# A recurrent attention and an MLP on one core: preparation once a chunk on dense tiles, moved within SBUF

## The chip, the cores and the metric

One core of a Trainium2 chip runs the kernel. Its engines work in parallel, each in the order of its own instructions, and wait for each other by semaphores: TensorE (PE; its weight loads are listed as PEld), VectorE (DVE), ScalarE (ACT), GpSimd (POOL) and SyncE (SP). SP does no arithmetic here: it issues DMAs, in order, and a DMA whose buffer is not yet free holds up all that stand behind it. GpSimd issues DMAs too. The metric is the device time in microseconds (us), lower is better.

## The reference, cut to what matters

A state of 40 x 40 for each of 4 batches and 8 heads is carried over 768 time steps; the outputs of all heads go through an MLP with Mish.

```python
# r, k, v, w, a, b: (4, 8, 768, 40)
for t in range(768):
    y[:, :, t] = einsum('bhd,bhde->bhe', rt, state)
    Sa = einsum('bhde,bhe->bhd', state, at)
    state = state * wt[:, :, None, :] - einsum('bhd,bhe->bhde', Sa, bt) \
            + einsum('bhd,bhe->bhde', vt, kt)
x = y.transpose(0, 2, 1, 3).reshape(3072, 320)
h = x @ w_in                                   # 320 -> 2048
g = h * tanh(softplus(h))                      # Mish
out = g @ w_out                                # 2048 -> 320
```

## The kernel before, in words

The 768 steps are cut into 12 chunks of 64 steps (C = 64, `nch` = 12). Within a chunk the recurrence is written with products: `P`, the running product of w, scales a; `E`, the products from the other end, scale b and k; and a 32 x 32 triangular inverse for each of 32 systems gives the effect of the Sa term. A chunk has 32 (batch, head) pairs. They are treated as two halves (`be` = 0, 1) of 16 pairs; in a half, `al` = 0, 1 stands on partitions 0 to 39 and 64 to 103, eight pairs s beside each other. So 80 of 128 partitions carry data.

The stages, by function:

- `pre_a(c, be)` prepares a half chunk. SP loads w and a (`wa`) and b and k (`bk`), VectorE forms the product of the first half of w (L145), the scan P (L147), a times P (L152), the scan E (L157) and b, k times E (L170). ScalarE copies a into a block-diagonal tile `ad` (L155). TensorE multiplies `ad` with `bk` (L186) and transposes `bk` (L202); ScalarE and VectorE bring the results into `GP` and `HA` (L188 to L193, the masks are VectorE's). Once a chunk TensorE moves the two ends of P to both halves (L166, with parts of the identity) into `RW`. GpSimd stores P to DRAM (`pD`, L172), since the MLP's input is y times P.
- `pre_inv(n)` inverts for two chunks at once: VectorE alone, from a transpose into `XL` (L209) over thirty pairs of product and sum (L214, L216) to a transpose into `TT` (L218) and one into GP (L220). `post_inv(n)` goes on with it on TensorE (L232, L241, L258).
- `step(c)` runs the recurrence of a chunk: products L284, L293, L304, L314, L334, L339, with VectorE at L316, L342, L346. GpSimd loads v and r for it.
- The MLP takes 256 rows for each chunk: products with w_in (L585), Mish, products with w_out (L605 to L607). Its weights arrive as pairs of 32-bit words, and are converted in parts: a DMA (`cv_d`, SP), ScalarE (L459), VectorE (L461 to L463), ScalarE (L494) and VectorE (L495). w_in takes twelve such parts of 512 columns. With `NQ0 = 1` three of them are converted at the program's start (`early`), into tiles of their own, the other nine when preparation's buffers are free (`first`), with one buffer (`CVA = 1`); w_out follows (`second`, `third`).

`ORDER` and `LA` set that preparation runs two pairs of chunks ahead of the steps. The order of the instructions on each engine is then set by a scheduler with its own estimate of durations; `OFF` shifts the priority of each part. `QS` names the engines that issue the DMAs of loads, step loads, outputs and P.

Of the kernel before, what the change touches and what calls it, by code (L numbers as in the profile page):

```python
# [7 lines left out]
F32 = mybir.dt.float32  # L8
# [10 lines left out]
NWA = 2  # L19
# [8 lines left out]
QS = "SGGG"  # L28
# [9 lines left out]
OFF = {'I': 80, 'T1': 80, 'P00': -40, 'P10': 80, 'P11': 40, 'b0': 15, 'c0': 600, 'u0': -15, 'u1': 250, 'd0': 250,  # L38
# [9 lines left out]
def layouts(inp, S=768):  # L48
# [7 lines left out]
    wt = w.transpose(4, 2, 1, 6, 3, 0, 5).reshape(nch, 2, 2, 40, 8, C)  # L56
    wa = np.zeros(wt.shape[:4] + (1040,), np.float32)
    wa[..., :520].reshape(wt.shape[:4] + (8, 65))[..., 1:] = wt
    wa[..., 528:] = a.transpose(4, 2, 1, 6, 3, 0, 5).reshape(nch, 2, 2, 40, 512)
    o['wa'] = wa  # L60
    bt, kt = (x.transpose(4, 2, 1, 6, 3, 0, 5).reshape(nch, 2, 2, 40, 8, 1, C) for x in (b, k))
    bk = np.concatenate([bt, kt], -2)
    bk[:, 1] = np.concatenate([kt, bt], -2)[:, 1]
    o['bk'] = bk.reshape(nch, 2, 2, 40, 8, 128)
# [4 lines left out]
    cst = np.zeros((128, 328), np.float32)  # L69
# [4 lines left out]
    cst[:, 296:328] = np.arange(32) < p[:, None] % 32  # L74
    o['cst'] = cst
# [3 lines left out]
def attention(ctx, tc, I, yD, pD, nch, M):  # L79
# [16 lines left out]
    cst = cs.tile([128, 328], F32, name="cst")  # L96
# [4 lines left out]
    wab = [cp.tile([128, 1040], F32, name=f"wa{i}") for i in range(NWA)]  # L101
    bkb = [cp.tile([128, 8, 168], F32, name=f"bk{i}") for i in range(NWA)]
    adb = [cp.tile([128, 8, 2, 2, 32], F32, name=f"ad{i}") for i in range(NAD)] * (2 // NAD)
    d1 = cp.tile([128, 584], F32, name="d1")
# [3 lines left out]
    for w, b in zip(wab, bkb):  # L108
        V.memset(w, 1.0)
        G.memset(b, 0.0)  # L110
    for t in [d1] + [x.rearrange("p s k a t -> p (s k a t)") for x in adb[:NAD]]:
        A.copy(t, z.broadcast_to(t.shape))
# [10 lines left out]
    RW, W2, HA, BKN, GP, KT = {}, {}, {}, {}, {}, {}  # L123
    LQ, SQ, OQ, PQ = (dict(S=SP, G=G, A=A)[x] for x in QS)

    def pre_a(c, be):
        n = 2 * c + be
        wa, bk, ad = wab[n % NWA], bkb[n % NWA], adb[n % 2]
        for al in range(2):
            q = slice(al * 64, al * 64 + 40)  # L130
            LQ.dma_start(out=wa[q], in_=I['wa'][c, be, al])
        for al in range(2):
            q = slice(al * 64, al * 64 + 40)
            LQ.dma_start(out=bk[q, :, 0:128], in_=I['bk'][c, be, al])
# [278 lines left out]

I32 = mybir.dt.int32
NH = 4
NQ0 = 1
NQ1 = 4
NO1 = 3
CVW = 512
# [240 lines left out]
```

## Time and profile before

| | us |
|---|---|
| median of 3 runs | 846.35 (843.54 to 848.62) |
| profiled execution | 842.54 |
| its span | 840.7 |
| TensorE busy, matmuls | 737.5 (88%) |
| VectorE busy | 463.3 (55%) |
| ScalarE busy | 427.9 (51%) |
| GpSimd busy | 103.3 (12%) |

In a line of the profile, L147 is a line of the kernel, `out<-in` are tiles without their buffer numbers, `x24` is the number of instructions, and behind the bar stand busy us, mean ns of one, and the idle time of the engine just before them with what ended it. Matmuls of 32-bit data are recorded twice, so eight products of a program show as x16. Granted clock 1.00 is TensorE's full speed; over the execution it was 0.947.

### The profile page before, as it was taken

Reading aid. Unit: us, or ns where it says so; the run is one execution under the profiler, and the core shown is the slowest. Engines: PE = TensorE matmul, PEld = TensorE weight load, DVE = VectorE, ACT = ScalarE, POOL = GpSimd, SP = SyncE. Lnnn points to the kernel's source line nnn. Section 1 sums busy time; section 2 is a strip of 40 time slices with the busy share of each in tenths; the row PEclk is TensorE's granted clock in tenths of the full one; section 3 lists DMA queues with packets and bytes.
Section 4 is the critical chain, followed back from the end, with each engine's and each line's share of the span. In section 5 each row is a group of like instructions: output and inputs, shape, how many; then the busy total and the mean of one; then the engine's idle time right before and its main releaser. Section 6 shows DMA issues by size and latency. Waiting matters only on the chain.

```text
span 840.7 us, 18817 instructions
## 1 busy us (share of the span) xinstructions
PE 737.5 (88%) x7816; PEld 688.5 (82%) x7816; DVE 463.3 (55%) x975; ACT 427.9 (51%) x937; POOL 103.3 (12%) x182
## 2 busy tenths in 40 slices
PE   2545898998989889888749999999999999999998
PEld 2444687887778778777648899999999999999998
DVE  6789889659879758947962649221222222122110
ACT  4533657774665766676457646333333333333331
POOL 8100021132123023211210200000000000000000
PEclk9755699899999999999978999999999999999999
DMA  6422232333333133313543744211120121100000
GB/s 173 139 72 64 82 78 67 96 75 94 89 96 88 57 86 98 96 26 98 139 123 82 186 132 127 54 39 32 38 54 29 26 54 36 35 20 16 16 1 32
DMA packets 58213, 61.92 MB, mean 74 GB/s; under 512 B 25536, under 2 KB 48704, under 8 KB 58128
## 3 DMA queue, kind: packets, MB, share of 16 engines
q1 hardware_dynamic: 49296, 40.94, 17.4%
q0 software_dynamic: 8832, 19.79, 9.4%
q8 instruction: 61, 1.00, 0.5%
q14 instruction: 24, 0.20, 0.1%
HBM read 48.79 MB, written 11.86 MB: 72 GB/s over the span
## 4 chain that ended last, share of the span: by engine, by line
PE 61%; ACT 15%; DVE 15%; DMA 5%; issue 4%; SPq 0%; POOL 0%; ACTq 0%; DVEq 0%
PE ph L585 20%; PE po L605 7%; PE po L606 7%; PE po L607 6%; PE pa L186 4%; PE pa L258 3%; PE pq L314 3%; PE pq L334 2%; DMA cv_d<-in_wi 2%; DVE XL L216 2%; DVE tmp L214 2%; ACT KT L260 2%; ACT bdT L250 1%; ACT bdT L249 1%; ACT ad L155 1%
## 5 line engine op out<-in xcount | busy, mean ns | idle before, releaser
L585 PE MATMUL ph<-xh,w_ih 128*128 128x256 f32 x576 | 148.9, 283 | 0.0
L587 ACT ACTIVATE g<-ph 128x512 f32<-128x512 f32 x96 | 57.3, 598 | 179.7 <-PE ph L585 179.7
L591 DVE TENSOR_TENSOR gl<-g,gh 128x1024 fp32r<-128x1024 f32 x48 | 58.6, 1224 | 160.3 <-ACT gh L590 160.0
L585 PE MATMUL ph<-xh,w_il 128*128 128x256 f32 x576 | 123.7, 283 | 0.0
L186 PE MATMUL pa<-bk,ad 128*128 128x168 f32 x384 | 85.5, 372 | 42.2 <-DVE bk L170 15.0
L606 PE MATMUL po<-w_ol,gh 128*128 128x320 f32 x384 | 118.6, 309 | 0.0
L607 PE MATMUL po<-w_oh,gl 128*128 128x320 f32 x384 | 118.3, 309 | 0.0
L605 PE MATMUL po<-w_oh,gh 128*128 128x320 f32 x384 | 117.8, 309 | 0.1
L585 PEld LDWEIGHTS ph<-xh,w_ih 128*128 128x128 f32 x576 | 109.5, 190 | 0.2 <-issue 0.2
L186 PEld LDWEIGHTS pa<-bk,ad 128*128 128x128 f32 x384 | 70.4, 232 | 47.6 <-issue 23.1
L585 PE MATMUL ph<-xl,w_ih 128*128 128x256 f32 x384 | 100.7, 284 | 0.0
L585 PEld LDWEIGHTS ph<-xh,w_il 128*128 128x128 f32 x576 | 96.2, 190 | 0.1
L585 PEld LDWEIGHTS ph<-xl,w_ih 128*128 128x128 f32 x384 | 73.1, 190 | 0.2 <-issue 0.2
L605 PEld LDWEIGHTS po<-w_oh,gh 128*128 128x128 f32 x384 | 71.8, 188 | 0.6 <-ACT w_oh L494 0.5
L606 PEld LDWEIGHTS po<-w_ol,gh 128*128 128x128 f32 x384 | 72.1, 188 | 0.2 <-DVE w_ol L495 0.2
L607 PEld LDWEIGHTS po<-w_oh,gl 128*128 128x128 f32 x384 | 72.1, 188 | 0.0
L216 DVE TENSOR_TENSOR XL<-XL,tmp 128x30 f32<-128x30 f32 (+9 forms) x180 | 58.8, 326 | 2.6
L214 DVE TENSOR_TENSOR tmp<-XL 128x30 f32<-128x30 f32 (+9 forms) x180 | 58.2, 323 | 2.6
L314 PE MATMUL pq<-bdr,UVT 128*128 128x128 f32 x384 | 55.2, 288 | 4.6 <-DVE UVQ L316 3.8
L258 PE MATMUL pa<-bdT,HA 128*104 128x128 f32 x384 | 52.7, 289 | 7.1 <-ACT bdT L251 4.8
L258 PEld LDWEIGHTS pa<-bdT,HA 128*104 128x104 f32 x384 | 47.2, 181 | 10.3 <-ACT bdT L251 5.9
L314 PEld LDWEIGHTS pq<-bdr,UVT 128*128 128x128 f32 x384 | 48.6, 197 | 7.0 <-DVE UVQ L316 4.9
(89 smaller groups left out, 1237.3 us busy)
## 6 DMA issues: line engine op xcount, KB each, us to landing
wa<-in_wa SPq DMA_DIRECT2D x48, 162.5 KB
bk<-in_bk SPq DMA_DIRECT2D x48, 160.0 KB
cv_d<-in_wi SPq DMA_DIRECT2D x12, 512.0 KB
cv_d<-in_wo SPq DMA_DIRECT2D x8, 640.0 KB
pD<-P POOLq DMA_DIRECT2D x48, 81.2 KB, 2.4
VS<-in_vN POOLq DMA_DIRECT2D x24, 160.0 KB, 3.3
UVT<-in_vD POOLq DMA_DIRECT2D x24, 160.0 KB, 4.0
bdr<-in_rD POOLq DMA_DIRECT2D x24, 160.0 KB, 4.5
```

The costliest lines, as they stand in the source:

```text
L186: PE.matmul(pt[:, j], ad[:, s0 + j].rearrange("p k a t -> p (k a t)"), bk[:, s0 + j], start=(j == 0), stop=True, skip_group_check=True)
L214: V.tensor_tensor(out=tv, in0=X[:, i + 1:32, i:i + 1].broadcast_to([128, 31 - i, i]), in1=X[:, i:i + 1, 0:i].broadcast_to([128, 31 - i, i] ...
L216: V.tensor_tensor(out=X[:, i + 1:32, 0:i], in0=X[:, i + 1:32, 0:i], in1=tv, op=ALU.add)
L258: PE.matmul(pk[:, j], ha[:, s0 + j], bd[:, s0 + j].rearrange("p a t -> p (a t)"), start=(j == 0), stop=True, skip_group_check=True)
L260: A.copy(kt[:, s0:s0 + 4], pk)
L314: PE.matmul(pq[:, s], UVT[:, g * 4 + s, be * 128:be * 128 + 128], br[:, be, g * 4 + s].rearrange("p a t -> p (a t)"), start=(s == 0), stop ...
L585: PE.matmul(o, w, x, start=(j == 0 and n == 0), stop=(n == 7), skip_group_check=True)
L587: A.activation(g[:, f0:f0 + 2], ph, AF.Mish)
L591: V.tensor_tensor(out=gl, in0=g, in1=gh.bitcast(F32), op=ALU.subtract)
L605: PE.matmul(po[k], gh[:, j, t], oh, start=(f == 0), stop=False, skip_group_check=True)
L606: PE.matmul(po[k], gh[:, j, t], ol, start=False, stop=False, skip_group_check=True)
L607: PE.matmul(po[k], gl[:, j, t], oh, start=False, stop=(f == 15), skip_group_check=True)
```

## The change

Preparation's work on VectorE is done once a chunk instead of once a half. `pre_d(c)` loads w, a, and b with k as dense tiles of 120 partitions and 11 blocks of 64 steps: three of the four groups of eight pairs (g = 2 be + al = 0, 1, 2) stand on partitions 0 to 39, 40 to 79 and 80 to 119, and the fourth group is spread over the three as blocks 8 to 10 (`wz`, `ax`, `bx`; two buffers each). The reduction, both scans and both products run on these. Then SP moves the results into the tiles that TensorE reads, by DMAs from SBUF to SBUF: six parts of a (into `a0`, `a1`, L178 of the new kernel) and six of b and k (into `bk0`, `bk1`, L184). P is stored by six DMAs a chunk instead of four (L193), and six selection products take the place of four (L189). The ScalarE copies, TensorE's products, the inverse and the steps stay as they were.

The MLP's weights are no longer converted early (`NQ0 = 0`): all twelve parts of w_in come in `first`, with two buffers (`CVA = 2`). `E` has a tile of its own, and the loads have a priority (`'L': 300`).

```diff
-NWA = 2
+NWZ = 2
+NAX = 2
+NBX = 2
+NE = 1
-QS = "SGGG"
+QS = "SGGGS"
...
-    def pre_a(c, be):
-        n = 2 * c + be
-        wa, bk, ad = wab[n % NWA], bkb[n % NWA], adb[n % 2]
-        for al in range(2):
-            q = slice(al * 64, al * 64 + 40)
-            LQ.dma_start(out=wa[q], in_=I['wa'][c, be, al])
-        for al in range(2):
-            q = slice(al * 64, al * 64 + 40)
-            LQ.dma_start(out=bk[q, :, 0:128], in_=I['bk'][c, be, al])
+    def parts():
+        for g in range(3):
+            yield g // 2, g % 2, slice(g * 40, g * 40 + 40), 0, 0, 8
+        for i in range(3):
+            yield 1, 1, slice(i * 40, i * 40 + 40), 8, 3 * i, min(3, 8 - 3 * i)
+
+    def pre_d(c):
+        wz = pw.tile([120, 716], F32, name="wz", bufs=NWZ)
+        a = pw.tile([120, 704], F32, name="ax", bufs=NAX)
+        bk = pw.tile([120, 11, 2, 64], F32, name="bx", bufs=NBX)
+        with at(tc, 'L'):
+            LQ.dma_start(out=wz, in_=I['wd'][c])
+            LQ.dma_start(out=a, in_=I['ad'][c])
+            LQ.dma_start(out=bk.rearrange("p s x t -> p (s x t)"), in_=I['bkd'][c])
...
+        V.tensor_reduce(out=w2[:, 0], in_=wz[:, 0:715].rearrange("p (s j) -> p s j", j=65)[:, :, 1:33], axis=AX.X, op=ALU.mult)
+        V.reciprocal(d1[:, 64:779:65], w2[:, 0])
+        V.tensor_tensor_scan(out=P, data0=wz[:, 0:715], data1=d1[:, 64:779], initial=0.0, op0=ALU.mult, op1=ALU.add)
...
         V.tensor_tensor(out=a3, in0=a3, in1=P3[:, :, 0:64], op=ALU.mult)
+        for be, al, q, h, s, m in parts():
+            DQ.dma_start(out=ab[be][al * 64:al * 64 + 40, s * 64:(s + m) * 64], in_=a[q, h * 64:(h + m) * 64])
+        V.reciprocal(d1[:, 64:779:65], w2[:, 1])
+        V.tensor_tensor_scan(out=E[:, 0:714][:, ::-1], data0=wz[:, 2:716][:, ::-1], data1=d1[:, 1:715][:, ::-1],
+                             initial=0.0, op0=ALU.mult, op1=ALU.add)
+        V.tensor_tensor(out=bk, in0=bk, in1=E3[:, :, 0:64].unsqueeze(2).broadcast_to([120, 11, 2, 64]), op=ALU.mult)
+        for be, al, q, h, s, m in parts():
+            DQ.dma_start(out=bkb[be][al * 64:al * 64 + 40, s:s + m, 0:128], in_=bk[q, h:h + m].rearrange("p s x t -> p s (x t)"))
+
+        RW[c] = wk.tile([128, 2, 16], F32, name="rw", bufs=4)
+        pt = ps_g.tile([128, 2, 2, 8], F32, name="pa")
+        for be, al, q, h, s, m in parts():
+            PE.matmul(pt[be * 64:be * 64 + 64, al, :, s:s + m], sel[:, q.start // 40], w2[:, :, h:h + m],
+                      start=(al == 0), stop=True, skip_group_check=True)
+        A.copy(RW[c], pt.rearrange("p a h s -> p a (h s)"))
+        for be, al, q, h, s, m in parts():
+            PQ.dma_start(out=pD[c, be, :, al, s * 65:(s + m) * 65], in_=P[q, h * 65:(h + m) * 65])
+
+    def pre_a(c, be):
+        if be == 0:
+            pre_d(c)
+        a, bk, ad = ab[be], bkb[be], adb[be]
...
-NQ0 = 1
+NQ0 = 0
...
-CVA = 1
+CVA = 2
```

The scheduler places the instructions anew. Line numbers of the new kernel from the inverse on are 29 higher than those of the old one (XL is L238, TT L247). On VectorE, ahead of the first inverse, there stood the last half of chunk 1 (`wa_97`, `bk_99`), a conversion (L461 to L495) and the masks (L191, L193); `w_689` belongs to chunk 2:

```order
L170 TENSOR_TENSOR bk_99<-bk_99,wa_97 128x8x128
L461 TENSOR_SCALAR cv_w<-cv_m 128x512
L462 SCALAR_TENSOR_TENSOR cv_w<-cv_m,cv_w 128x512
L463 SCALAR_TENSOR_TENSOR cv_w<-cv_d,cv_w 128x512
L191 TENSOR_TENSOR HA<-pa,cst 128x3x64
L145 TENSOR_REDUCE w_689<-wa_96 128x8
L495 SCALAR_TENSOR_TENSOR w_il_928<-cv_w,w_ih_927 128x512
L191 TENSOR_TENSOR HA<-pa,cst 128x3x64
L191 TENSOR_TENSOR HA<-pa,cst 128x2x64
L193 TENSOR_TENSOR GP<-GP,cst 128x8x32
L146 RECIPROCAL d_102<-w_689 128x8
L209 STREAM_TRANSPOSE XL<-GP 128x32x32
```

Now stand there the ends of chunk 3 (`w_823`), the first scan of chunk 4 (`w_1100`, L171) and the masks of both halves of chunk 1 (L220, L222):

```order
L176 TENSOR_TENSOR ax<-ax,P 120x704
L171 SCALAR_TENSOR_TENSOR P<-wz,d_96 120x715
L220 TENSOR_TENSOR HA<-pa,cst 128x3x64
L174 COPY w_1100<-P 120x11
L179 RECIPROCAL d_96<-w_1100 120x11
L220 TENSOR_TENSOR HA<-pa,cst 128x3x64
L222 TENSOR_TENSOR GP<-GP,cst 128x8x32
L220 TENSOR_TENSOR HA<-pa,cst 128x2x64
L220 TENSOR_TENSOR HA<-pa,cst 128x3x64 x2
L222 TENSOR_TENSOR GP<-GP,cst 128x8x32
L220 TENSOR_TENSOR HA<-pa,cst 128x2x64
L238 STREAM_TRANSPOSE XL<-GP 128x32x32
```

The conversion is gone from that place, and two to three later chunks have moved ahead of the inverse; the masks of chunk 1 stand behind chunk 4's scan.

On SP, in the new kernel, this is the stretch with chunk 1's moves (`ax_255`, `bx_256`). `wz_1092` is chunk 4's load of w, and takes the buffer that chunk 2's scans read; `ax_816` belongs to chunk 3 and `wz_1219` to chunk 5:

```order
L160 DMA bx_690<-in_bkd 120x1408
L178 DMA a0_90<-ax_255 40x512 x2
L178 DMA a1_91<-ax_255 40x512
L178 DMA a1_91<-ax_255 40x192
L158 DMA wz_1092<-in_wd 120x716
L178 DMA a1_91<-ax_255 40x192
L178 DMA a1_91<-ax_255 40x128
L184 DMA bk0_92<-bx_256 40x8x128 x2
L159 DMA ax_816<-in_ad 120x704
L158 DMA wz_1219<-in_wd 120x716
L184 DMA bk1_93<-bx_256 40x8x128
L184 DMA bk1_93<-bx_256 40x3x128 x2
```

In the old kernel SP held loads alone, in the order of the halves; the moves of a chunk now stand between the loads of later ones, and chunk 1's moves of b and k (L184) behind chunk 4's load.

On VectorE at the end of the last inverse, the old kernel had conversions on both sides of TT (L218):

```order
L216 TENSOR_TENSOR XL<-XL,tmp 128x2x29
L214 TENSOR_TENSOR tmp<-XL 128x30
L216 TENSOR_TENSOR XL<-XL,tmp 128x30
L495 SCALAR_TENSOR_TENSOR w_il_5097<-cv_w,w_ih_5096 128x512
L218 STREAM_TRANSPOSE TT<-XL 128x32x32
L220 STREAM_TRANSPOSE GP<-TT 64x32x32
L461 TENSOR_SCALAR cv_w<-cv_m 128x512
L462 SCALAR_TENSOR_TENSOR cv_w<-cv_m,cv_w 128x512
L463 SCALAR_TENSOR_TENSOR cv_w<-cv_d,cv_w 128x512
L495 SCALAR_TENSOR_TENSOR w_il_5129<-cv_w,w_ih_5128 128x512
L461 TENSOR_SCALAR cv_w<-cv_m 128x512
L462 SCALAR_TENSOR_TENSOR cv_w<-cv_m,cv_w 128x512
```

In the new one the last pairs of the inverse stand by themselves up to TT (L247), and work on the MLP's input x (L596 to L599) follows; no conversion of w_in is left behind TT:

```order
L245 TENSOR_TENSOR XL<-XL,tmp 128x2x29
L243 TENSOR_TENSOR tmp<-XL 128x30
L245 TENSOR_TENSOR XL<-XL,tmp 128x30
L247 STREAM_TRANSPOSE TT<-XL 128x32x32
L596 TENSOR_TENSOR xy<-xy,xp 128x768
L249 STREAM_TRANSPOSE GP<-TT 64x32x32
L598 TENSOR_TENSOR xl<-xy,xh 128x512
L599 TENSOR_TENSOR xh<-xy,xh 64x256
L596 TENSOR_TENSOR xy<-xy,xp 128x768
L345 TENSOR_TENSOR UVQ_113<-pq,cst 128x8x64
```

All twelve conversions of w_in now stand ahead of TT: two of them open ahead of the last XL (L238), ten between XL and TT, where the old kernel had six. On TensorE the order around the last inverse is as it was: two full steps, then the products with TT, and the first products of the MLP behind those.

84 lines of the change are left out of this document (38 added, 46 removed).

## The prediction

> **What bounds the kernel now.** I read the stages first: the busy time of each engine between the marks that the inverses set. Columns: stretch, its length, busy us (and instructions) of TensorE's matmuls, its weight loads, VectorE, ScalarE, GpSimd; granted TensorE clock, share of the DMA engines, GB/s.
>
> ```profile
> span 840.7 us, 18817 instructions
> 0.00:48.70 48.70, 23.04 (x111) 19.57 (x112) 34.40 (x67) 25.46 (x65) 19.55 (x36) 0.86 0.53 145
> 48.70:100.50 51.80, 28.41 (x180) 23.24 (x178) 48.38 (x120) 21.60 (x63) 5.08 (x10) 0.62 0.23 68
> 100.50:383.50 283.00, 254.29 (x3592) 222.75 (x3592) 214.89 (x534) 189.19 (x495) 58.20 (x105) 0.97 0.31 80
> 383.50:432.40 48.90, 33.49 (x514) 29.61 (x512) 44.50 (x115) 24.99 (x54) 13.96 (x21) 0.97 0.52 144
> 432.40:500.00 67.60, 61.01 (x877) 57.05 (x878) 29.79 (x48) 40.70 (x81) 6.49 (x10) 0.89 0.43 112
> 500.00:840.70 340.70, 337.23 (x2550) 336.32 (x2548) 91.31 (x97) 125.97 (x181) 0.00 (x0) 1.00 0.15 42
> ```
>
> Five sixths of the program are TensorE's: 90% busy from 100 to 383 us (254.3 of 283.0), 90 and 99% after 432. VectorE bounds two stretches. In the first inverse it is busy 48.4 of 51.8 us and TensorE 28.4. In the last inverse it is busy 44.5 of 48.9 and TensorE 33.5. The timeline gives the marks: the first product of preparation, the transposes that open (XL) and close (TT) the first and last inverse, and TensorE's wait for the last one.
>
> ```profile
> 14.96 4.84 PE L186 MATMUL pa<-bk,ad 128*128 128x168 f32 x16 [14.96 <-DVE bk L170]
> 48.73 2.10 DVE L209 STREAM_TRANSPOSE XL<-GP 128x1024 f32<-128x1024 f32 x1
> 95.91 1.94 DVE L218 STREAM_TRANSPOSE TT<-XL 128x1024 f32<-128x1024 f32 x1
> 100.48 2.11 DVE L209 STREAM_TRANSPOSE XL<-GP 128x1024 f32<-128x1024 f32 x1
> 383.50 2.14 DVE L209 STREAM_TRANSPOSE XL<-GP 128x1024 f32<-128x1024 f32 x1
> 430.51 1.89 DVE L218 STREAM_TRANSPOSE TT<-XL 128x1024 f32<-128x1024 f32 x1
> 432.46 1.92 PE L232 MATMUL pa<-TT,GP 32*32 32x32 f32 x64 [7.28 <-DVE TT L218]
> ```
>
> TensorE ran out of work at 425.2 and stood 7.28 us for the last inverse. Between 100 and 383 its waits are short and mostly ScalarE's, as the list of waits of that stretch shows (total us, times, longest):
>
> ```profile
> PE pu L293 <- ACT UVT L286: 5.8, 4, 3.2
> PE pa L202 <- ACT bkn L203: 5.6, 6, 1.2
> PE pa L258 <- ACT bdT L251: 3.9, 5, 1.4
> ...
> PE pa L232 <- DVE TT L218: 2.1, 4, 0.7
> ```
>
> So a microsecond saved on VectorE counts before 100 us and between 383 and 432, and little between.
>
> **Dense tiles: VectorE's work.** The groups by line (busy us, mean ns) price a half chunk:
>
> ```profile
> L147 DVE TENSOR_TENSOR_SCAN P<-wa,d 128x520 f32<-128x520 f32 x24 | 29.6, 1235 | 0.3
> L157 DVE TENSOR_TENSOR_SCAN wa<-wa,d 128x519 f32<-128x519 f32 x24 | 29.6, 1233 | 6.8 <-ACT ad L155 6.7
> L170 DVE TENSOR_TENSOR bk<-bk,wa 128x1024 f32<-128x1024 f32 x24 | 29.1, 1212 | 1.4 <-DMA bk<-in_bk 1.3
> ...
> L152 DVE TENSOR_TENSOR wa<-wa,P 128x512 f32<-128x512 f32 x24 | 16.4, 682 | 0.0
> ...
> L145 DVE TENSOR_REDUCE w<-wa 128x8 f32<-128x256 f32 x24 | 9.8, 409 | 1.9 <-DMA wa<-in_wa 1.4 <-PE pa L166 0.4
> ...
> L146 DVE RECIPROCAL d<-w 128x8 f32<-128x8 f32 x24 | 4.8, 199 | 0.2
> ```
>
> With three small instructions at 0.2, a half costs 1.235 + 1.233 + 1.212 + 0.682 + 0.409 + 0.6 = 5.37 us and a chunk 10.74. The products grow by (1212 - 682)/512 = 1.035 ns an element, which gives 0.88 us for 704 and 1.61 for 1408, and 0.51 for the reduction over 352. A scan of 715 lies between 1.44 (that slope) and 1.70 (in proportion); I take 1.65, nearer to the second, since a scan of 520 already takes twice a product of that size. A dense chunk is then 0.51 + 0.6 + 3.3 + 0.88 + 1.61 = 6.9 us, and twelve chunks save 46 us of VectorE.
>
> **The first stage.** By the order, VectorE had 36.9 us ahead of the first XL (four halves, three conversions of 2.5, the masks) and 51.5 from there to TT. Now 35 us (nearly five dense chunks run ahead) and 40. Were that all, TT would come 13 us sooner; this is the lower bound, -13. Against it stand the ways that a chunk now takes. The moves of chunk 0 stand in SP's queue behind 2.98 MB (two chunks of 1.36 MB, 0.27 of constants).
>
> ```profile
> 2.00:4.00 2.00, 0.00 (x0) 0.00 (x0) 0.93 (x1) 1.99 (x4) 2.00 (x3) 1.00 0.98 307
> 6.00:8.00 2.00, 0.00 (x0) 0.00 (x0) 1.93 (x4) 0.13 (x1) 2.00 (x2) 1.00 0.73 204
> ...
> pD<-P POOLq DMA_DIRECT2D x48, 81.2 KB, 2.4
> ...
> L172 POOL DMA_DIRECT2D pD<-P x48 | 25.0, 525 | 164.5 <-DVE w L150 94.9 <-DVE tmp L214 37.0 <-DVE XL L216 11.5
> ```
>
> At 307 GB/s (while loads of 128 rows ran) the constants land near 12 us, at 204 (loads of 40 rows) near 17; I take 14, between the rates since the new loads have 120 rows. A move within SBUF has no row; the nearest is the store of P, 2.4 us to landing, and I take that (0 and 4.8, twice it, as ends). Then chunk 0's first product starts near 17 instead of 14.96. The Trainium skill ("DMA: Bandwidth & Descriptors", section "Why a DMA increments its semaphore by 16 and not by 1") says that a DMA runs on the largest number of engines up to 16 that divides its outer size, which is 10 for 40 rows and 15 for 120; the shares of 0.73 and 0.98 above agree. By it the new loads would run near the upper rate, the constants would land some 2 us sooner than I take, and the sum below would be 854; but each move has 40 rows, and would be held to 10 engines.
>
> Two waits follow. On SP, chunk 4's load of w stands ahead of chunk 1's moves of b and k and waits for chunk 2's second scan (near 29.5 us); behind it wait those moves, and for them TensorE, which starts chunk 1 near 34.5. On GpSimd, six stores a chunk in place of four (525 ns each) hold P's buffer for chunk 4: VectorE's scan waits about 2 us for them, and the masks of chunk 1 stand behind it. The first XL comes near 51, 2 us late. From there 40 us of VectorE and some 3 us of waits for chunk 2, whose moves stand behind chunk 6's load in the same manner, put TT near 94. Term: -2, between -13 and +6 (none of VectorE's relief through, both queues 4 us worse).
>
> **The middle.** The relief of 7.7 us a pair of chunks lies beside TensorE. What it can end are waits like VectorE's row in the list above and part of ScalarE's, which come behind VectorE's masks and TT: -4, between 0 and -10. Added on TensorE: six selections a chunk for four.
>
> ```profile
> L166 PE MATMUL pa<-w,cst 128*64 128x16 f32 x96 | 5.0, 214 | 1.6 <-ACT bkn L203 1.5
> ```
>
> That is 24 more of two records; 5.0/48 = 0.104 us each gives +2.5 (between 0 and 24 x 2 x 0.214 = 10). The moves' cost here is hidden as long as preparation runs a pair ahead, as the order has it; without that cover each chunk would pay one landing of 2.4 us.
>
> **No early weights: the last inverse.** One conversion on VectorE is 0.459 + 0.686 + 0.685 + 0.684 = 2.51 us:
>
> ```profile
> L461 DVE TENSOR_SCALAR cv_w<-cv_m 128x512 int32<-128x512 int32 x12 | 5.5, 459 | 14.2 <-ACT cv_m L459 14.1
> L462 DVE SCALAR_TENSOR_TENSOR cv_w<-cv_m,cv_w 128x512 int32<-128x512 int32 x12 | 8.2, 686 | 0.2
> L463 DVE SCALAR_TENSOR_TENSOR cv_w<-cv_d,cv_w 128x512 int32<-128x512 int32 x12 | 8.2, 685 | 0.2
> L495 DVE SCALAR_TENSOR_TENSOR w_il<-cv_w,w_ih 128x512 fp32r<-128x512 f32 x12 | 8.2, 684 | 4.5 <-ACT w_ih L494 4.5
> ```
>
> Before, six of the twelve stood between the last XL and TT, three came early and three after. By the new order all but the first part of two stand there, 26.5 us for 15.1, and one set of the MLP's x besides (768, 512 and 256 elements, by the slope above 0.95 + 0.68 + 0.42 = 2.05); the steps lose 0.9. VectorE then has 60.9 us between XL and TT where it had 48.3, that is +12.6, and TensorE has nothing to run meanwhile: in its order the products of the MLP still follow the last inverse. The second buffer for conversions cannot take more away than VectorE's idle time of that stretch, 48.9 - 44.5 = 4.4; two loads at once may be late instead. Term: +13, between +8 and +20. The three conversions that leave the stretch after TT lay beside a busy TensorE: 0, at most -3.
>
> **Sum.** The profiled execution took 842.54 us (span 840.7). 842.54 - 2 - 4 + 2.5 + 13 = 852; the median of the three runs, 846.35, is 3.8 above that execution, so 856.
>
> **The rivals.** Faster: VectorE was what held the start and the inverses, and its relief goes through. For it speaks 48.4 of 51.8 us in the first inverse; against it that VectorE was idle for 14.3 of the 48.7 us ahead of the first XL. It gives -13 and, with all of the middle's bound, -10, against +2.5 and +13: 839. It decides once TT of the first inverse comes before 88 us. No change: the last inverse opens some 12 us sooner against TensorE's last two steps, so that those cover the conversions; against it, XL needs chunk 11's last products, and what TensorE still has to run behind these (383.5 to 425.2, 42 us) is by the counts in the new order about the same. With the start as I have it: 846.35 - 2 - 4 + 2.5 + 1 = 844. Much slower: SP's in-order waits also reach TensorE in the middle, one landing of 2.4 us for each of eight chunks, +19: 875; for it speaks that loads and moves of three chunks alternate in one queue, against it the pair of lead.
>
> **How the numbers follow.** The forecast has 0.42 (own range 849 to 864), faster 0.27, no change 0.19, much slower 0.12. A measurement of this kernel tells about 0.5% from no change, 842.1 to 850.6. Faster by more: 0.27. Within: 0.21 (the no-change case and the forecast's edge). Slower: 0.52. From 835 to 871 no more than 2 in 10 is left out: half of the much slower case and the ends of the faster one.
>
> **What would show it.** VectorE's busy time falls by some 46 us. The first XL stands near 51 and TT near 94; the scan of chunk 4 is preceded by a wait for GpSimd's stores. From XL of the second inverse to XL of the last it takes 280 us, give or take 5. From the last XL to TT it takes 60 to 64 us, and TensorE's wait before the first product with TT is 18 to 22 us for 7.28. I am wrong if that wait stays below 12, if TT of the first inverse comes before 88, or if waits of TensorE for moves (bk or ad by DMA) sum to over 10 us in the middle.

## The result, and the profile after

| | before | after |
|---|---|---|
| median, us | 844.94 (843.03 to 848.62, 4 runs) | 877.9 (874.04 to 884.73, 4 runs) |
| ratio, 95% interval | | 1.0393 (1.0313 to 1.0474) |
| profiled execution, us | 842.54 | 884.73 |
| VectorE busy, us | 463.3 | 432.8 |
| granted clock | 0.947 | 0.921 |

The changed kernel is slower by 33 us in the medians, where 10 were forecast. Its profiled execution is the slowest of its four, so the stages below add up to 42.3 us and not to 33. The first fence has the stretches between the inverses' marks, with the prediction's columns; the second has the marks. In the table, "XL" and "TT" are the transposes that open and close an inverse, and "the middle" is the part from the second XL to the last.

```profile
span 883.0 us, 18960 instructions
0.00:60.60 60.60, 25.23 (x116) 21.76 (x116) 33.52 (x55) 23.40 (x61) 31.23 (x60) 0.77 0.77 189
60.60:110.00 49.40, 28.56 (x266) 24.23 (x264) 42.05 (x100) 22.22 (x66) 6.05 (x12) 0.69 0.48 128
110.00:410.20 300.20, 263.17 (x3670) 231.51 (x3672) 188.77 (x466) 191.63 (x503) 60.98 (x110) 0.94 0.37 96
410.20:473.40 63.20, 34.10 (x396) 30.28 (x392) 56.40 (x134) 27.10 (x56) 11.21 (x16) 0.74 0.50 134
```

```profile
20.89 4.19 PE L215 MATMUL pa<-bk,ad 128*128 128x168 f32 x16 [3.32 <-DMA bk<-bx]
60.62 2.13 DVE L238 STREAM_TRANSPOSE XL<-GP 128x1024 f32<-128x1024 f32 x1
102.91 1.94 DVE L247 STREAM_TRANSPOSE TT<-XL 128x1024 f32<-128x1024 f32 x1
109.97 2.13 DVE L238 STREAM_TRANSPOSE XL<-GP 128x1024 f32<-128x1024 f32 x1
410.19 2.18 DVE L238 STREAM_TRANSPOSE XL<-GP 128x1024 f32<-128x1024 f32 x1
471.47 1.91 DVE L247 STREAM_TRANSPOSE TT<-XL 128x1024 f32<-128x1024 f32 x1
473.44 1.92 PE L261 MATMUL pa<-TT,GP 32*32 32x32 f32 x64 [20.79 <-DVE TT L247]
```

| part of the program, us | before | after | difference | forecast |
|---|---|---|---|---|
| start to second XL | 100.5 | 110.0 | +9.5 | -2 |
| second XL to last XL | 283.0 | 300.2 | +17.2 | -1.5 |
| last XL to TT | 47.0 | 61.3 | +14.3 | +13 |
| TT to the end | 410.2 | 411.5 | +1.3 | 0 |

In the middle TensorE idled 300.20 - 263.17 = 37.0 us for 28.7 before, and was busy 8.9 us longer, with 78 more records than 3592 and at a lower granted clock (0.94 for 0.97). VectorE was busy 188.8 us for 214.9 there, so its relief is real and bought nothing. Another trace of nearly the same order of instructions (e3 below) has 297.0 us there, so some 3 of the 17 are this execution's. The list of waits of the middle (total us, times, longest) says what stood instead. Waits on SP are waits in its queue.

```profile
PE pq L363 <- DVE UVQ L345: 14.4, 4, 5.4
...
DVE bx L182 <- DMA bx<-in_bkd: 14.6, 5, 5.3
...
SPq L184 <- PE pa L231: 85.1, 9, 27.4
SPq L178 <- ACT ad L201: 53.8, 9, 26.8
...
SPq L160 <- DMA bk<-bx: 7.5, 3, 4.3
```

VectorE stands at the product with bx because its load is late; UVQ stands behind that product in VectorE's order, and TensorE's L363 waits 14.4 us for UVQ. Before, the same two waits were 1.3 and 0.9 us:

```profile
DVE bk L170 <- DMA bk<-in_bk: 1.3, 2, 0.7
PE pq L334 <- DVE UVQ L316: 0.9, 2, 0.6
```

The longest of them shows the chain: VectorE waits for the load, then runs the product, then UVQ, and then TensorE goes on.

```profile
270.71 1.62 DVE L182 TENSOR_TENSOR bx<-bx,E 120x1408 f32<-120x1408 f32 x1 [2.92 <-DMA bx<-in_bkd]
274.40 0.68 DVE L345 TENSOR_TENSOR UVQ<-pq,cst 128x512 f32<-128x512 f32 x1
275.14 1.13 PE L363 MATMUL pq<-UVQ,bkn 128*64 128x104 f32 x10 [5.44 <-DVE UVQ L345]
```

No move is waited for by TensorE itself in this stretch: the page counts 18.9 us of such waits, and the list of waits up to 110 us has all of them.

```profile
L215 PE MATMUL pa<-bk,ad 128*128 128x168 f32 x384 | 82.6, 365 | 29.5 <-DMA bk<-bx 18.9 <-DVE HA L220 7.4 <-ACT bkn L232 2.8
```

```profile
PE pa L215 <- DMA bk<-bx: 18.9, 3, 11.8
```

In the start (up to the second XL) the chunks' way is longer. Rows: start, duration, what was issued or run, and the idle time before it.

```profile
8.92 4.65 SPq L178 DMA_DIRECT2D a<-ax  x6
15.92 5.14 SPq L184 DMA_DIRECT2D bk<-bx  x6
...
16.54 1.03 PE L189 MATMUL pa<-w,cst 120*64 120x16 f32 x12 [16.54 <-DMA cst<-in_cst]
...
36.45 1.63 DVE L180 TENSOR_TENSOR_SCAN E<-wz,d 120x714 f32<-120x714 f32 x1
...
38.10 0.34 SPq L158 DMA_DIRECT2D wz<-in_wd  x1
...
40.09 1.65 SPq L184 DMA_DIRECT2D bk<-bx  x2
...
44.98 3.70 PE L215 MATMUL pa<-bk,ad 128*128 128x168 f32 x12 [3.81 <-DMA bk<-bx]
```

Six moves take SP 4.65 to 5.14 us to issue, some 0.8 each, where a load takes 0.4. Chunk 4's load of w goes out at 38.10, as chunk 2's scan E ends, and chunk 1's last moves behind it, as forecast, but 9 us later than forecast.

### The profile page after: what moved, and what is told of

It reads as the page before. It is cut to its first block, busy times and chain, and to the rows that moved or that the text cites. A ratio compares the mean times of both kernels' runs of the same rounds, so it can differ in the third digit from the quotient of the medians.

```text
span 883.0 us, 18960 instructions
## 1 busy us (share of the span) xinstructions
PE 748.7 (85%) x7864; PEld 701.1 (79%) x7864; DVE 432.8 (49%) x877; ACT 426.6 (48%) x937; POOL 116.0 (13%) x208
## 3 DMA queue, kind: packets, MB, share of 16 engines
q1 hardware_dynamic: 55596, 53.27, 22.4%
## 4 chain that ended last, share of the span: by engine, by line
PE 61%; DVE 12%; ACT 11%; DMA 10%; issue 3%; SPq 2%; POOL 1%; DVEq 0%; ACTq 0%
PE ph L614 21%; PE po L635 6%; PE po L634 6%; PE po L636 6%; PE pq L363 4%; PE pa L215 3%; PE pq L343 3%; PE pa L287 3%; DMA bx<-in_bkd 2%; DMA cv_d<-in_wi 2%; DMA bk<-bx 2%; PE pq L368 2%; PE pa L231 2%; DVE tmp L243 1%; DMA ax<-in_ad 1%
## 5 line engine op out<-in xcount | busy, mean ns | idle before, releaser
L215 PE MATMUL pa<-bk,ad 128*128 128x168 f32 x384 | 82.6, 365 | 29.5 <-DMA bk<-bx 18.9
L614 PE MATMUL ph<-xl,w_ih 128*128 128x256 f32 x384 | 100.7, 284 | 0.0
L363 PE MATMUL pq<-UVQ,bkn 128*64 128x104 f32 (+1 forms) x768 | 51.9, 280 | 19.7 <-DVE UVQ L345 15.9
L343 PE MATMUL pq<-bdr,UVT 128*128 128x128 f32 x384 | 59.2, 295 | 4.8 <-DVE UVQ L345 3.0
L363 PEld LDWEIGHTS pq<-UVQ,bkn 128*64 128x64 f32 x768 | 43.4, 155 | 23.6 <-DVE UVQ L345 17.2
```

The lines of the kernel that those rows point to most:

```text
L215: PE.matmul(pt[:, j], ad[:, s0 + j].rearrange("p k a t -> p (k a t)"), bk[:, s0 + j], start=(j == 0), stop=True, skip_group_check=True)
L343: PE.matmul(pq[:, s], UVT[:, g * 4 + s, be * 128:be * 128 + 128], br[:, be, g * 4 + s].rearrange("p a t -> p (a t)"), start=(s == 0), stop ...
L363: PE.matmul(py[be * 64:be * 64 + 64, 2 * j + al, 0:n], BKN[c, be][:, u * 40:u * 40 + 64], UVQ[be][:, u, 0:n], start=(j == 0 and al == 0), ...
L614: PE.matmul(o, w, x, start=(j == 0 and n == 0), stop=(n == 7), skip_group_check=True)
```

## The experiments

The theory after the first look: three parts, namely the conversions in the last inverse, the chunk's longer way in the start, and in the middle a queue on SP in which loads stand behind moves that wait for TensorE. All comparisons are with the kernel before in the same set of runs. A row named "before" edits the kernel before; every other row edits the changed kernel. The marks (us) are read from each trace as above; "last XL" is the time of the start and the middle together.

| run | ratio (95%) | second XL | last XL | last XL to TT | TensorE's wait for TT | TT to end |
|---|---|---|---|---|---|---|
| before | 1 | 100.5 | 383.5 | 47.0 | 7.3 | 410.2 |
| after | 1.039 (1.031 to 1.047) | 110.0 | 410.2 | 61.3 | 20.8 | 411.5 |
| e1 before, weights' part | 1.019 (1.012 to 1.026) | 104.4 | 388.6 | 66.4 | 21.5 | 409.2 |
| e18 before, second buffer | 1.022 (1.019 to 1.025) | 100.2 | 387.4 | 64.9 | 17.7 | 410.9 |
| e11 before, w_in after TT | 1.020 (1.015 to 1.026) | 100.3 | 385.1 | 28.0 | 2.0 | 446.7 |
| e15 before, three ahead | 1.004 (1.001 to 1.007) | 100.4 | 384.7 | 36.7 | 1.0 | 423.8 |
| e16 before, four ahead | 1.002 (0.999 to 1.005) | 96.6 | 384.3 | 42.9 | 2.0 | 419.6 |
| e2 loads on GpSimd | 1.024 (1.019 to 1.030) | 124.0 | 396.9 | 60.9 | 21.0 | 413.1 |
| e3 constants second | 1.039 (1.033 to 1.046) | 108.5 | 405.5 | 60.3 | 20.4 | 410.0 |
| e4 three buffers | 1.033 (1.027 to 1.038) | 117.9 | 404.0 | 60.3 | 20.4 | 409.7 |
| e5 moves of a on ScalarE | 1.041 (1.036 to 1.046) | 116.1 | 401.2 | 65.9 | 21.5 | 411.6 |
| e6 later loads on GpSimd | 1.049 (1.041 to 1.057) | 105.5 | 401.0 | 62.5 | 20.9 | 413.9 |
| e7 early quarter | 1.028 (1.020 to 1.036) | 111.5 | 399.7 | 56.1 | 19.4 | 411.0 |
| e17 early, one buffer | 1.024 (1.021 to 1.027) | 112.4 | 406.1 | 47.7 | 11.6 | 414.0 |
| e8 e5, e6, e7 together | 1.030 (1.025 to 1.035) | 109.7 | 403.0 | 56.3 | 19.7 | 410.9 |
| e10 w_in after TT | 1.021 (1.016 to 1.026) | 107.0 | 405.6 | 32.2 | 0.9 | 426.9 |
| e12 early, rest after TT | 1.016 (1.012 to 1.019) | 113.9 | 405.2 | 29.9 | 0.9 | 424.4 |
| e9 one-row moves | 1.022 (1.018 to 1.026) | 103.5 | 388.8 | 62.0 | 20.5 | 411.2 |
| e13 one-row, early | 1.022 (1.017 to 1.027) | 106.1 | 390.5 | 58.3 | 19.3 | 411.5 |
| e14 four one-row moves | 1.028 (1.022 to 1.034) | 100.7 | 393.8 | 63.1 | 20.1 | 414.3 |

Repeated runs of one kernel differ by up to 11 us (the changed kernel: 874 to 885). The middle of the kernel before, with the same number of TensorE's records and 28 to 30 us of idle time each time, took 283.0 us at a granted clock of 0.97, and 287.2 and 287.7 at 0.95 (e18, e16). So a mark of one trace within some 5 us of another says little; ratios and marks are to be read together.

### e1: the weights' part alone

In the kernel before:

```diff
-NQ0 = 1
+NQ0 = 0
...
-CVA = 1
+CVA = 2
```

> The kernel before with one part of the change alone: no weights converted early, two conversion buffers (NQ0 = 0, CVA = 2); preparation is the old one. Theory (conversions between the last XL and TT cost VectorE's time, and TensorE waits for TT): from the last XL to TT 58 to 62 us for 47.0, TensorE's wait before the first product with TT 18 to 22 us for 7.3, ratio to the kernel before 1.010 to 1.016 (some 854 to 858 us). Rival 1 (the longer last inverse is dense preparation's fault: XL late against TensorE's steps): XL to TT near 48, ratio 0.995 to 1.003. Rival 2 (the early conversions held up the start, so that taking them out gives back as much): the last inverse longer, but the first XL some 8 us sooner and the ratio near 1.00.

As the theory had it, and a little more: XL to TT is 66.4 us, TensorE's wait 21.5, and the loss 18.7 us in the medians. More than half of the whole loss comes without dense preparation.

### e2 to e6: the queue

e2 and e6 give GpSimd the loads, e4 gives them a third buffer; e5 moves a by ScalarE, e3 loads the constants sooner. Each is one edit in the changed kernel.

```diff
-QS = "SGGGS"
+QS = "GGGGS"        # e2
...
-            LQ.dma_start(out=cst, in_=I['cst'])
+                LQ.dma_start(out=cst, in_=I['cst'])    # e3, behind chunk 0's load of w
...
-NWZ = 2             # and NAX, NBX
+NWZ = 3             # e4
...
-            DQ.dma_start(out=ab[be]...
+            A.dma_start(out=ab[be]...    # e5
...
+            L2 = LQ if c < 2 else G      # e6, issues the three loads
```

> The changed kernel with preparation's loads issued by GpSimd; the moves stay on SP. Theory (loads stand in SP's queue behind moves that wait for TensorE's transposes, and VectorE stands at the product with bx for them): VectorE's wait for the load of bx falls from 15.5 us in all to under 5, TensorE's wait at L363 for UVQ from 14.4 to under 5, second XL to last XL from 300 to some 287, total 10 to 14 us below the changed kernel's 878 (ratio to the kernel before 1.022 to 1.028). Rival 1 (the moves' own landing and their wait for TensorE hold the chunks): the wait for bx goes, but second XL to last XL stays within 4 us of 300 and the ratio at 1.035 to 1.045. Rival 2 (GpSimd's own in-order waits take SP's place): the waits move to the loads of w and the ratio is 1.03 or more.

> The changed kernel with the constants loaded second (after chunk 0's w) and not behind 3 MB of loads. Theory (the start is late because the constants are: SP and ScalarE wait for them, and the moves of chunk 0 stand behind): the first product of preparation at 15 to 17 us for 20.9, the first XL at 55 to 57 for 60.6, total 3 to 6 us below the changed kernel. Rival (the start is late because of the moves and VectorE's in-order waits for later loads): the first product sooner, but the first XL within 1.5 us of 60.6 and no gain.

> The changed kernel with three buffers for w, a and b with k as loaded (NWZ = NAX = NBX = 3 for 2). Theory (a load that is issued a chunk sooner has landed when SP is blocked): VectorE's wait for the load of bx in the middle falls to under 5 us, second XL to last XL to some 288, the first stage some 3 us shorter (chunk 4's load no longer waits for chunk 2's scan), total 10 to 16 us below the changed kernel. Rival (moves themselves, landing and order): the wait for bx goes, and the time is within 4 us of the changed kernel.

> The changed kernel with the six moves of a issued by ScalarE; loads and the moves of b with k stay on SP. Theory (a move costs SP 0.8 us of issue, twelve a chunk, and that sets the first stage): the first product of preparation at 17 to 18.5 us for 20.9, the first XL at 55 to 57 for 60.6, the second near 104 for 110; in the middle SP no longer waits for ScalarE's copies, so second XL to last XL some 290; ratio to the kernel before 1.018 to 1.026 (the changed kernel: 1.033 to 1.04). Rival 1 (landing, not issue, sets the start): first product within 1 us of 20.9 and first XL at 60 or later. Rival 2 (ScalarE now waits in order for VectorE's product and for buffers, and its copies behind them): a middle of 300 or more and a ratio of 1.035 or more.

> The changed kernel with the loads of chunks 0 and 1 on SP and of all later chunks on GpSimd. Theory (with all loads on GpSimd the start was late only because they stood behind GpSimd's clearing of tiles; what the middle won was SP's queue): first product near 21, second XL near 110 as in the changed kernel, second XL to last XL 272 to 282 as with all loads on GpSimd, ratio 1.010 to 1.018. Rival (the middle was short with all loads on GpSimd only because a later start let steps run ahead of the second XL): second XL near 110, second XL to last XL 290 or more, ratio 1.022 or more.

e2 came mostly as expected: VectorE's wait for bx fell to 7.8 us (under 5 was expected), TensorE's at L363 for UVQ to 1.9, and it lies some 13 us below the changed kernel's ratio, although its start is later (the first loads now stand behind GpSimd's clearing of tiles: first product at 30.2).

```profile
PE pq L363 <- DVE UVQ L345: 1.9, 3, 0.7
...
DVE bx L182 <- DMA bx<-in_bkd: 7.8, 4, 3.8
```

e3 fell: with the constants in time TensorE's first product still waited for moves (21.2). e4 is half a hit: its middle is 286.1, with a wait for bx of 11.0 where under 5 was expected, but the loads that run ahead now stand before the moves of chunks 0 and 1, and the second XL is 8 us later. e5 and e6 missed. Both shorten the middle (285.2, 295.5) and end no sooner than the changed kernel; with e6 the first XL stood at 50.5, and the next 55.0 us later. In e6 its rival came true: the later loads are off SP's queue as in e2, and VectorE's wait for bx is 13.7 us again. So taking the loads off SP is not enough by itself, and a part of e2's short middle may be only its late start. An edit that moves one DMA queue also moves the order in which everything else is issued, so these runs do not isolate SP's queue.

### e9: the moves' bytes

Each move carries one row for forty; the other 39 are left out. The traces have the same instructions in the same order on every engine as the changed kernel's. This is the cleanest of the comparisons. Bytes, packets and time to landing fall together in it, so "bytes" below stands for all three.

```diff
-DQ.dma_start(out=ab[be][al * 64:al * 64 + 40, ...], in_=a[q, ...])
+DQ.dma_start(out=ab[be][al * 64:al * 64 + 1, ...], in_=a[q.start:q.start + 1, ...])
```

(and the same for b with k.)

> The changed kernel whose twelve moves a chunk each carry one row for forty; the other 39 rows are left out (TensorE multiplies what stands in the tiles), every issue, wait and product stays, and so does the order of the instructions. Theory now (it is the way of a move that counts: landing and DMA queue time of 0.72 MB a chunk, not the issue): first product at 17 to 18.5 us for 20.9, TensorE's wait for the moves of b and k before 110 us from 18.9 to under 8, second XL at 101 to 104 for 110, total 6 to 12 us below the changed kernel, ratio 1.024 to 1.032. Rival (what costs is SP's issue of 0.8 us for each of twelve moves, and its in-order waits): first product and second XL within 1.5 us of the changed kernel's, ratio 1.035 or more.

By the tiles' sizes the moves carry 0.98 MB a chunk, not the 0.72 of that text. Without them the hardware queue moves 41.77 MB for 53.27. The rows are its stretches, its waits in the middle, and the queue of the changed kernel and of this one (packets, MB, share of 16 engines):

```profile
0.00:56.00 56.00, 22.57 (x116) 19.77 (x116) 33.29 (x55) 23.15 (x61) 31.26 (x60) 0.82 0.69 163
56.00:103.50 47.50, 26.19 (x254) 22.65 (x252) 41.91 (x99) 21.05 (x64) 6.05 (x12) 0.75 0.32 80
103.50:388.80 285.30, 256.70 (x3682) 225.09 (x3684) 188.24 (x465) 192.86 (x505) 60.98 (x110) 0.98 0.31 77
388.80:452.80 64.00, 35.35 (x400) 31.35 (x394) 56.70 (x134) 27.20 (x57) 11.22 (x16) 0.74 0.49 133
```

```profile
PE pq L363 <- DVE UVQ L345: 4.7, 3, 2.6
...
DVE bx L182 <- DMA bk<-bx: 4.7, 1, 4.7
DVE bx L182 <- DMA bx<-in_bkd: 2.2, 3, 1.1
...
SPq L184 <- PE pa L231: 88.6, 10, 25.9
SPq L178 <- ACT ad L201: 52.8, 9, 24.6
```

```profile
q1 hardware_dynamic: 55596, 53.27, 22.4%
```

```profile
q1 hardware_dynamic: 38988, 41.77, 18.3%
```

The middle is 285.3 us, nearly the 283.0 of the kernel before, and the wait for bx's load is nearly gone. SP's waits are as long as ever. So it was not that SP stands behind TensorE, as my theory and my much-slower rival had it, but the time that 0.98 MB a chunk takes on the way. Of the 14.9 us that the middle is shorter, 8.4 are TensorE's idle time (28.6 for 37.0). The other 6.5 are its busy time, at a clock of 0.98 for 0.94; that the moves lower the clock is not shown, since traces of the kernel before's own middle differ by 4 to 5 us with the clock (above). A move that takes longer frees bx's buffer later (the waits of SP's L160 above), and lies ahead of the next load in the queue; which of the two counts more is not separated. A third buffer (e4) and another queue (e2) each shortened VectorE's wait. Nor do the bytes make the load late in every order: e7, e12 and e17 below carry all 40 rows, wait at most 0.7 us for bx's load in the middle, and leave TensorE idle for 27.7 to 29.5 us there. The first product came at 19.2 and the second XL at 103.5, so the bytes are 6.5 of the start's 9.5 us. The ratios of the two kernels give 0.0175 x 846 = some 15 us for the bytes, with their intervals 7 to 22.

### e14: the moves' number

Four moves a chunk in place of twelve, of one row each; all other rows are left out.

```diff
+            if al == 0:      # ahead of each move of one row
```

> The changed kernel with four moves a chunk in place of twelve (one of a and one of b with k into each half's tile), of one row each; all other rows are left out. Theory (what remains of the late start with one-row moves is SP's issue of twelve moves, 0.8 us each): first product at 15.5 to 17.5 us for 19.2 with twelve one-row moves, second XL at 97 to 100 for 103.5, ratio 1.012 to 1.018. Rival (it is the chain through VectorE's scans, the moves and their waits, however few): first product within 1 us of 19.2, second XL at 102 or later, ratio 1.019 to 1.026.

It ends between the two. The start nearly came (first product 18.3, first XL 48.2, second XL 100.7), the time did not: the instructions stand in another order, and the middle is 293.1. No wait explains that: TensorE is idle for 27.6 us there, less than in e9, and busy for longer at a granted clock of 0.94. Why the clock was lower is open. The rest of the late start goes with fewer moves, but that their issue is its cause is not shown.

### e7, e13, e8: the early quarter again

The early quarter fits with E written into w's tile and parts of 128 columns; it has a low priority (`'E': -400`) and one conversion buffer (`CVE = 1`).

```diff
-NQ0 = 0
+NQ0 = 1
...
+CVWE = 128           # columns of an early part
...
-        E = pw.tile([120, 715], F32, name="E", bufs=NE)
+        E = wz[:, 2:717]
```

> The changed kernel with a quarter of the weights converted early again, in twelve parts of 128 columns and at a low priority, most of them in the middle (NQ0 = 1, CVE = 1; E is written into w's tile to make room). Theory (the last inverse is long because of its conversions): last XL to TT 52 to 55 us for 61.3, TensorE's wait before the first product with TT 11 to 15 us for 20.8, the middle within 4 us of the changed kernel's, ratio 1.024 to 1.031. Rival (the conversions cost as much where VectorE and SP's queue are in use as in the last inverse): last XL to TT shorter by as much, the middle longer by 6 to 10, ratio 1.035 or more.

> The kernel with a quarter of the weights converted early (parts of 128 columns) and with moves of one row for forty; the other rows are left out. Theory (two separate parts make the loss, the moves' bytes some 13 us and the weights some 8 to 18, and VectorE's relief is worth next to nothing): ratio 1.006 to 1.015, second XL near 105, the middle no longer than before's 283 by more than 4. Rival 1 (VectorE's relief comes out once both are gone): ratio 0.985 to 0.998. Rival 2 (the two parts are one, the same wait seen twice): ratio 1.018 or more.

> The changed kernel with three edits together: loads of chunks 2 and later on GpSimd, the moves of a on ScalarE, a quarter of the weights converted early in parts of 128 columns. Theory (three separate costs, each of which its edit takes away): second XL near 104, second XL to last XL near 277, last XL to TT near 53, ratio 0.995 to 1.008. Rival (VectorE's relief is worth nothing beside the moves, and one wait takes another's place): ratio 1.015 or more.

In e7 XL to TT fell to 56.1 and the ratio to 1.028, about as expected, but TensorE's wait for TT stayed at 19.4 for 11 to 15: TensorE was through with what it had left 38.7 us after XL, for 42.5, at a granted clock up to then of 0.96 for 0.84. With one-row moves the early quarter gave nothing (1.022 for e9's 1.022), which was rival 2. e18 offers a reason: the early quarter was not what had been lost. Beside the early quarter one-row moves gave little (e13 1.022, e7 1.028, with intervals that overlap), so the 15 us of e9 hold for the changed kernel's order. e8 missed; three remedies did not add up (second XL 109.7 for 104, middle 293.3 for 277).

### e18, e17: the second buffer

```diff
-CVA = 1
+CVA = 2              # e18: alone, in the kernel before
```

e17 is e7 with `CVA = 1`.

> The kernel before with a second conversion buffer (CVA = 2) and nothing else; the early quarter stays. By the order all nine late conversions then stand between the last XL and TT, for six. Theory: last XL to TT 54 to 58 us for 47.0, TensorE's wait 14 to 18 for 7.3, ratio 1.008 to 1.014, that is over half of the 1.019 that the whole change of the weights' part costs alone. Rival (the missing early quarter is the cost): last XL to TT 47 to 50, ratio 0.997 to 1.004.

> The changed kernel with a quarter of the weights converted early in parts of 128 columns, as in e7, but with one conversion buffer for the rest (CVA = 1). By the order six conversions stand between the last XL and TT, as in the kernel before, for seven with two buffers and ten in the changed kernel. Theory (the second buffer is part of the cost): last XL to TT 50 to 53 us for 56.1, TensorE's wait before the first product with TT 10 to 14 for 19.4, ratio 1.018 to 1.024. Rival (the second buffer costs nothing; the last inverse opens later against TensorE's work whatever the conversions): TensorE's wait 17 us or more, ratio 1.026 or more.

In the kernel before this settles whose the weights' part is. The second buffer alone costs 19.5 us, as much as e1's whole edit; that the early quarter is gone added nothing that can be told from noise. The stretch of the last inverse of e18 and of e17 (its third row), and TensorE's first product with TT:

```profile
387.40:454.30 66.90, 38.60 (x514) 34.58 (x513) 53.32 (x131) 29.27 (x62) 14.12 (x21) 0.81 0.56 144
```

```profile
454.30 1.92 PE L232 MATMUL pa<-TT,GP 32*32 32x32 f32 x64 [17.70 <-DVE TT L218]
```

```profile
406.10:455.80 49.70, 31.42 (x398) 28.16 (x394) 44.38 (x114) 22.99 (x49) 11.12 (x16) 0.84 0.43 119
```

In e18 nine conversions and one set of the MLP's x stand between XL and TT where six did, 8.8 us more of VectorE (53.32 for the 44.5 of before), and VectorE idles 13.6 us there for 4.4, among it 4.9 for ScalarE's part of the conversions and 2.7 for the load of P. With one buffer and the early quarter in the changed kernel (e17) XL to TT is 47.7, as before, and the ratio 1.024. What is left, some 21 us, lies in the start and the middle: it is dense preparation's own, though e17 also has E in w's tile, and what that costs is not separated. The second buffer's own price there is not clear of noise (e7 1.028, e17 1.024, with intervals that overlap).

### e10, e11, e12, e15, e16: the conversions behind TT

Each conversion buffer is first written from TT, so that w_in's conversions wait for the last inverse.

```diff
+    if hold:
+        V.tensor_copy(d.bitcast(F32)[:, 0, 0:1], hold.pop())     # hold: TT, once a buffer
     SP.dma_start(out=d.rearrange("p a b -> p (a b)"), in_=src.bitcast(I32))
```

e10 has it in the changed kernel, e11 in the kernel before, e12 in e7; e15 and e16 leave the first three and four of the kernel before free.

> The changed kernel with every conversion of w_in held until TT of the last inverse (each conversion buffer is first written from TT). Theory (conversions between XL and TT are what TensorE waits for in the last inverse): last XL to TT 33 to 39 us for 61.3, TensorE's wait before the first product with TT under 3 for 20.8, the twelve conversions then lie beside steps 10 and 11 at a cost of 0 to 6, ratio 1.014 to 1.024. Rival 1 (they only move the wait: the MLP's first products wait for weights): TT sooner by 25, the end sooner by under 8, ratio 1.030 or more. Rival 2 (the last steps wait for VectorE behind the conversions): the same, with TensorE's waits at L363 for UVQ.

> The kernel before with the same hold: its nine late conversions of w_in wait for TT of the last inverse. Theory: last XL to TT 33 to 38 us for 47.0, TensorE's wait of 7.3 goes, ratio 0.986 to 0.996, so the version that beats both. Rival (the time is only moved behind TT): ratio 0.998 to 1.006.

> The changed kernel with a quarter converted early in parts of 128 columns and the other nine conversions held until TT. Theory (the weights' part of the loss is gone, preparation's part of start and middle is left): last XL to TT near 36, TensorE's wait under 3, ratio 1.008 to 1.018; what is left over 1.00 is preparation's, with the second XL near 111 for 100.5. Rival (dense preparation costs nothing, all was the weights): ratio 0.995 to 1.003.

> The kernel before, with three of its nine late conversions of w_in free and the other six held until TT (it had six ahead of TT). Theory (between TensorE's wait of 7.3 us at six and the MLP's wait for weights at none lies a place with neither): last XL to TT 38 to 41 us for 47.0, TensorE's wait there under 1, no new wait over 3 behind it, ratio 0.990 to 0.996. Rival (each conversion held costs the MLP's start as much as it saves): ratio 0.998 or more.

> The kernel before, with four of nine late conversions free and five held until TT. Theory: last XL to TT 40 to 43 us, TensorE's wait under 2, ratio 0.991 to 0.997. Rival: 0.998 or more.

In the changed kernel the hold does what was hoped: TT comes 32.2 us after XL, with a wait of 0.9, and of the 29 us that this is sooner 15.4 are given back behind TT. With the early quarter as well (e12) the ratio is 1.016, the best with dense preparation and as expected: what is left lies ahead of the last XL, at 405.2 for 383.5.

```profile
439.80 1.20 PE L261 MATMUL pa<-TT,GP 32*32 32x32 f32 x64 [0.87 <-DVE TT L247]
```

In the kernel before it loses: TT comes 17.4 us sooner and the end takes 36.5 longer, among it 9.1 us in which TensorE waits for the MLP's x.

```profile
PE ph L591 <- ACT xh L574: 9.1, 1, 9.1
```

With three or four conversions ahead the wait at TT is 1 or 2 us for 7.3, and the time is 1.004 and 1.002: it has only moved, as the rivals of e15 and e16 had it. No version tried beats the kernel before.

## Why the prediction was wrong, point by point

The step that failed is the price of the moves within SBUF: one landing of 2.4 us at the start, and nothing in the middle. Taking their bytes away (e9) gives back some 15 of the 33 us; the start and the middle, forecast at -3.5 us together, came at +26.7 in the profiled execution.

- Right: slower, and the last inverse, by its own working and not by luck. XL to TT was 61.3 (60 to 64 forecast), TensorE's wait 20.8 (18 to 22), and it had 452.65 - 410.19 = 42.5 us left to run (42). Ten whole conversions and the last step of two more stood there, as its sum of 26.5 us has them, and VectorE's records there add up to 60.9 us, as forecast, for 48.5 before. (Its busy time is less, 56.4 for 44.5 in the stretches above, since records overlap.) What this step did not see is why the conversions stood there. It puts them down to the missing early weights, and asks of the second buffer only what it can "take away", at most 4.4 us. In the kernel before the second buffer alone does it (e18), since it lets conversions of later parts, and the MLP's x, stand ahead of TT.
- Wrong: the first stage, -2 with bounds of -13 and +6; it came +9.5. The term that was mis-sized is the moves' way, taken from a store of P, 2.4 us to landing. That row has neither the load that they put on the DMA queue nor 0.8 us of issue each. One-row moves give back 6.5 us. The first XL stood at 60.6 for 51 and the first TT at 102.9 for 94, both signs that the prediction had named; its three conditions for being wrong, none of which came true, did not include a late start. VectorE's row there is right in sign (75.6 us busy to the second XL for 82.8) and had nowhere to go: TensorE's first product at 20.89 waited for moves, the next for masks behind a late load.
- The constants landed at 16.5, for the 14 taken; with the constants there in time TensorE's first product was as late (e3). Between 2 and 14 us the rate was 211 to 256 GB/s, mostly nearer to the 204 of 40 rows than to the 307 of 128. Two of these rows (the last two columns: share of the DMA engines, GB/s):

```profile
4.00:6.00 2.00, 0.00 (x0) 0.00 (x0) 1.38 (x3) 0.76 (x1) 2.00 (x4) 1.00 0.98 238
6.00:8.00 2.00, 0.00 (x0) 0.00 (x0) 1.97 (x3) 0.00 (x0) 2.00 (x3) 1.00 0.92 211
```

  The Trainium skill ("DMA: Bandwidth & Descriptors", section "Why a DMA increments its semaphore by 16 and not by 1") puts 120 rows on 15 engines by its rule, and the prediction read from it a rate near the upper one. The shares of 0.92 and 0.98 are near 15 of 16 (0.94), while the 0.73 of 40 rows, which the prediction called agreement, lies above 10 of 16 (0.63). The rate is not near 307, so the number of engines alone does not give it.
- Wrong: the middle, -1.5; it came +17.2 in the slowest execution (+14 by e3's trace). "Hidden as long as preparation runs a pair ahead" counts the landing of a move and not what the moves do to the loads behind them: VectorE waits 14.6 us for bx's load, and TensorE 14.4 behind it. e9 shows this part, with the same order: 285.3 us, and waits of 2.2 and 4.7. Where a clock of 0.94 for 0.97 adds to it, the cause stays open.
- The much slower rival (875, at 0.12) comes near the time by luck: it puts all of it in the middle, and the start lost 9.5 as well. Its mechanism, TensorE waiting one landing a chunk for moves behind SP's in-order waits, is not what happened: the list of waits of the middle has no wait of TensorE for a move, and SP's waits stay as they are when the time is won back (e9).
- VectorE's saving was forecast 46 us. The records of preparation's eight lines sum to 85.5 us for 128.0, so 42.5; its busy time fell by 30.5, since records that overlap count once there (all of its records sum to 510.8 us before and 467.0 after, for 463.3 and 432.8 busy).
- Chunk 4's scan did wait for GpSimd's stores, 2.7 us for the 2 forecast.

The parts do not add up to the whole. Dense preparation with the weights' part undone costs 21 us (e17), the weights' part on the old preparation 19 (e1, e18), both together 33. One-row moves with the weights' part undone, and one buffer, were not run, so what dense preparation would cost without both is open.

## What to carry to other kernels

Work that is taken off an engine which does not bound a stage pays only if what replaces it is free, and a move within SBUF is not: it stands in the same queue as the loads, so price it by what it does to the transfer behind it and to the engine that waits in order for that transfer. A second buffer lets a filler task run ahead of a critical chain on the same in-order engine: count which instructions it lets stand there before calling it harmless. Where a wait is removed, look behind the next join; three times here the time had only moved.

## What the runs showed of the hardware

- The issue of one move within SBUF takes SP 0.8 us with 40 rows (4.65 us for six, 5.14 for the next six) and still 0.7 with one row, where a load of 120 rows takes 0.4. In e9's timeline:

```profile
1.27 0.34 SPq L159 DMA_DIRECT2D ax<-in_ad  x1
...
8.92 4.17 SPq L178 DMA_DIRECT2D a<-ax  x6
```

- The granted clock was low in TensorE's wait for the last inverse: 0.53 in the changed kernel (20.8 us), 0.65 in e18 (17.7), 0.80 in the kernel before (7.3). In e18 it was low ahead of that wait too. The same 514 records took 33.5 us at 1.00 in the kernel before and 38.6 at 0.86 in e18, and 33.5 / 0.86 = 39, so the clock accounts for the difference. They ran before the wait, so it is not that wait that slowed them; TensorE's other idle time there was 8.2 and 10.6 us, and the cause of the lower clock is not shown. First the row of the kernel before, then that of e18:

```profile
383.50:425.20 41.70, 33.49 (x514) 29.61 (x512) 38.38 (x101) 22.40 (x49) 11.19 (x17) 1.00 0.51 140
387.40:436.60 49.20, 38.60 (x514) 34.58 (x512) 39.27 (x94) 27.13 (x57) 11.36 (x17) 0.86 0.55 151
```
